# Gate rows as columns through DRAM, gate weights behind the filters, and inverse tables scaled on GpSimd, in a one-core AdaLN, spectral filter and SwiGLU block

## The chip, the cores and the metric

One core of a Trainium2 chip. The metric is the device time of one execution in microseconds (us). The kernel before takes 252.17 us (median of four runs, 251.6 to 252.89). An execution is called slow when it is over 1.5% above the fastest of the same kernel, otherwise fast. Each run also comes with the mean clock that the throttle granted TensorE.

## The reference, cut to what matters

```python
x = A_x                                                  # (1, 2048, 640), bf16
mod = (silu(c) @ w_mod).reshape(1, 6, 1, 640)            # w_mod (640, 3840)
sa, ca, ga, sb, cb, gb = mod[:, 0], ..., mod[:, 5]
h = layernorm(x) * (1 + ca) + sa
x = x + ga * irfft2(rfft2(h) * (w_r + 1j * w_i))         # the spectral half
h = layernorm(x) * (1 + cb) + sb
x = x + gb * ((silu(h @ w_gate) * (h @ w_up)) @ w_down)  # the gated half, FF = 1728
```

`ga` and `gb` are rows of 640 numbers. The kernel needs each on all 128 partitions: `ga` to scale the table `RI` of the inverse transform, `gb` to scale `w_down`. `sb` and `cb` are needed as columns (five groups of 128).

## The kernel before

Stages, with times of its profile: forward transform to 35.5 us; the spectral stretch, 21 groups of frequencies, each with products by the filters on VectorE, to 60.3 us; the change-over to 64.8 us; the inverse, 16 token tiles at a pitch of 1.1 us, to 82.3 us; then gate/up and down projections to 249.1 us. The first of five transposed tiles of the second layer norm (`h2T`) is made during the inverse: VectorE normalises two token tiles, the Sync queue issues a transpose by DMA, GpSimd and ScalarE multiply and add (`1+cb`, `sb`), and gate/up starts on it.

```python
# loads on the Sync queue, in order (cut)
#  ... wm_r[:, :, 0] (the ga weights, 800 KB), the filters Wv by way of DRAM, Ktab,
#  four DMA transposes of the spectral data, then:
nc.sync.dma_start(wm_r[:, :, 1:3, :], wm_m[:, :, 1:3, :])
nc.sync.dma_start(wm_r[:, :, 3, :], wm_m[:, :, 3, :])
nc.sync.dma_start(Htab[:], H_dram)
nc.sync.dma_start(RI[:], RI_dram)
#  ... w_down, the last columns of gate and up (Wp13), gate/up

def mod_bc(j, lo, bank, o=0, ks=range(NC5)):          # a gate row, on all partitions at once
    gps_ = psum[:, bank, o:o + 320]
    for k in ks:
        nc.tensor.matmul(gps_, lhsT=sc_rep[:, k, :], rhs=wm_r[:, k, j, lo:lo + 320], start=(k == 0), stop=(k == NC5 - 1))
    return gps_
# ga: two calls ahead of the first groups, copied by ScalarE to ga_bc [P, 4, 160]
# sb, cb: one-column products inside groups NG-4 .. NG-1, copied by VectorE

# the change-over
    if g == NG - 1:
        rot(40, 8, slice(0, 64), nc.vector, (1,))
        nc.vector.tensor_tensor(RI[:, 1], RI[:, 1], ga_bc[:], ALU.mult)      # fold 1
for l0, n, i in rots:
    rot(l0, n, slice(0, 64), nc.gpsimd, (i,))
nc.scalar.copy(gb_bc[:, 320:640], mod_bc(3, 320, 3, 128))
s1em(0); s1em(1)                                       # H-table products of tiles 0 and 1
for q0, q1 in ((0, 8), (8, 32), (32, 64)):
    rot(64, 16, slice(q0, q1), nc.vector)
nc.vector.tensor_tensor(RI[:, 0], RI[:, 0], ga_bc[:], ALU.mult)              # fold 0
```

`rot` multiplies by plus or minus one (a rotation by the imaginary unit). "Fold" below is the scaling of a half of `RI` by `ga`.

## Time and profile before

| kernel before, profiled run of 250.93 us, clock 1.0 | us |
|---|---|
| span | 249.12 |
| first filter product, last one ends | 37.81, 60.26 |
| first inverse matmul | 64.75 |
| first three gate/up loads issued | 63.0, 65.7, 67.7 |
| transpose of the first `h2T` tile issued, its first use | 71.83, 77.80 |
| first gate/up matmul, and from there to the end | 82.38, 166.74 |

This execution is 1.2 us faster than the median of the kernel before. The last row divides the kernel: what follows the first gate/up matmul is the same program before and after.

### The profile page before, as it was taken

The page shows a single profiled execution, that of the slowest core. Times are in us where ns is not written, and L with a number is a line of the kernel's source. Part 1 is how long each engine was busy: PE and PEld are TensorE (multiplying, and loading weights), DVE is VectorE, ACT ScalarE, POOL GpSimd, SP SyncE. Part 2 cuts the span into 40 slices and gives each one's busy share as a digit, 9 for nine tenths or more (in the row PEclk, how much of TensorE's full clock was granted, in tenths as well). Part 3 has the DMA queues.
Part 4 walks back from the last instruction along what each step waited for, and adds up shares of the span by engine and source line. Part 5 has one row for each costly group of instructions (what it writes and reads, how often), then busy time and mean ns, then how long its engine had stood idle before and what let it go on. Part 6 is the DMA issues. An engine that isn't in the chain of part 4 may idle for free.

```text
span 249.1 us, 6473 instructions
## 1 busy us (share of the span) xinstructions
PE 243.5 (98%) x2512; PEld 200.4 (80%) x2512; DVE 209.7 (84%) x524; ACT 162.7 (65%) x300; POOL 74.3 (30%) x122
## 2 busy tenths in 40 slices
PE   8999999999999999999999999999999999999994
PEld 3778877999889888688877778886768887779973
DVE  4798888998898997879997997879995888895895
ACT  3778666997788798488862487674356766235740
POOL 8487755894025422000003900001330000440000
PEclk9999999999999999999999999999999999999999
DMA  7999999999999999300005020003311000211001
GB/s 221 396 357 334 309 365 191 175 397 381 286 352 288 275 264 186 81 9 0 3 0 108 13 68 29 3 3 58 73 42 39 3 0 3 54 53 57 3 0 53
DMA packets 45760, 34.43 MB, mean 138 GB/s; under 512 B 21731, under 2 KB 42658, under 8 KB 45346
## 3 DMA queue, kind: packets, MB, share of 16 engines
q1 hardware_dynamic: 43936, 30.00, 42.8%
q0 software_dynamic: 1504, 3.95, 6.7%
q8 instruction: 19, 0.31, 0.5%
q10 hardware_dynamic: 290, 0.08, 0.1%
q14 instruction: 11, 0.09, 0.1%
HBM read 26.72 MB, written 4.72 MB: 126 GB/s over the span
## 4 chain that ended last, share of the span: by engine, by line
PE 80%; SPq 9%; DMA 6%; ACT 1%; DVE 1%; issue 1%; DVEq 0%; ACTq 0%
PE psum L1016 33%; PE psum L899 19%; PE psum L986 9%; DMA rW<-wflip_r 4%; PE psum L879 3%; PE psum L597 3%; PE psum L664 3%; PE psum L567 2%; SPq L273 2%; SPq L277 2%; PE psum L1149 2%; DMA rM<-in_w_mod_dram 2%; SPq L275 2%; PE psum L1152 2%; PE psum L974 2%; PE psum L618 2%
## 5 line engine op out<-in xcount | busy, mean ns | idle before, releaser
L1016 PEld LDWEIGHTS <-rW 128*128 128x128 bf16 (+1 forms) x528 | 46.9, 98 | 5.6 <-issue 0.2
L1016 PE MATMUL psum<-rW 128*128 128x256 bf16 (+1 forms) x240 | 27.1, 259 | 0.0
L913 POOL TENSOR_TENSOR rM<-rM,rL 128x320 f32<-128x320 f32 x6 | 5.9, 975 | 68.2 <-ACT rL L912 68.2
L899 PEld LDWEIGHTS <-rE 128*128 128x128 f16 (+1 forms) x196 | 19.1, 97 | 7.7
L1016 PE MATMUL psum<-rY,rW 128*128 128x256 bf16 (+1 forms) x96 | 24.0, 259 | 0.0
L986 PE MATMUL psum<-rW 128*128 128x256 bf16 (+1 forms) x170 | 23.1, 291 | 0.0
L899 PE MATMUL psum<-rE 128*128 128x320 f16 (+1 forms) x147 | 22.3, 299 | 0.0
L590 DVE TENSOR_TENSOR rM<-psum,rW 128x384 bf16<-128x384 f32 (+2 forms) x42 | 20.1, 541 | 2.0 <-PE psum L567 1.4
L986 PEld LDWEIGHTS <-rW 128*128 128x128 bf16 x170 | 16.6, 98 | 3.8
L1016 PEld LDWEIGHTS <-rE 128*128 128x128 f16 x192 | 17.4, 98 | 2.4
L899 PEld LDWEIGHTS <-rX 128*128 128x128 bf16 (+1 forms) x151 | 14.6, 97 | 5.4
L760 POOL TENSOR_TENSOR rstd<-rstd,mhalf 128x4 f32<-128x4 f32 (+2 forms) x4 | 4.5, 1120 | 48.2 <-DVE rstd L756 48.2
L1052 DVE TENSOR_TENSOR rH<-psum,rW 128x512 bf16<-128x512 f32 x21 | 14.5, 689 | 4.9 <-PE psum L1016 3.1
L1048 ACT COPY rH<-psum 128x512 f32<-128x512 f32 x21 | 12.3, 585 | 9.0 <-PE psum L1016 7.3
L1042 ACT COPY rW<-psum 128x512 f32<-128x512 f32 x21 | 12.3, 585 | 6.8 <-PE psum L1016 6.7
L1055 ACT COPY rX<-psum 128x512 f32<-128x512 f32 x21 | 12.3, 586 | 6.7 <-PE psum L1016 6.7
L1070 DVE TENSOR_TENSOR rX<-rH,rL 128x512 bf16<-128x512 bf16 x21 | 8.9, 423 | 9.1 <-ACT rL L1068 9.0
L382 DVE SCALAR_TENSOR_TENSOR rE<-rE,mv,psum 128x648 bf16<-128x648 f32 (+1 forms) x17 | 14.2, 844 | 2.1 <-PE psum L318 1.5
L1056 DVE TENSOR_TENSOR rX<-psum,rX 128x512 f32<-128x512 f32 x21 | 14.4, 685 | 1.7 <-ACT rX L1055 1.6
L899 PE MATMUL psum<-rA,rX 128*128 128x320 bf16 (+1 forms) x98 | 15.6, 299 | 0.0
L1016 PE MATMUL psum<-rH,rW 128*128 128x256 f16 (+1 forms) x96 | 15.1, 259 | 0.1
L1016 PE MATMUL psum<-rE,rY 128*128 128x256 f16 (+1 forms) x96 | 15.1, 259 | 0.0
(198 smaller groups left out, 674.3 us busy)
## 6 DMA issues: line engine op xcount, KB each, us to landing
out_dram<-rA SPq DMA_DIRECT2D x31, 80.0 KB, 1.6
rM<-in_w_mod_dram SPq DMA_DIRECT2D x3, 800.0 KB, 9.9
rX<-in_A_x_dram SPq DMA_DIRECT2D x3, 640.0 KB, 7.3
rA<-in_B_w_down_dram SPq DMA_DIRECT2D x2, 960.0 KB, 14.4
rM<-in_w_mod_dram SPq DMA_DIRECT2D x1, 1600.0 KB, 7.1
rY<-in_B_w_gate_dram POOLq DMA_DIRECT2D x2, 768.0 KB, 7.7
rW<-in_B_w_gate_dram SPq DMA_DIRECT2D x2, 640.0 KB, 7.2
rW<-in_B_w_up_dram SPq DMA_DIRECT2D x2, 640.0 KB, 6.5
```

The costliest lines, as they stand in the source:

```text
L382: nc.vector.scalar_tensor_tensor(Zv[:, h], Cv[:, h], mv[:, t, 0:1], zps[:, h], ALU.mult, ALU.subtract)
L590: nc.vector.tensor_tensor(PP[:, :, hl], xv[:, :, hl], in1, ALU.mult)
L597: nc.tensor.matmul(yps[:, i, :], lhsT=_rev(PP, 64 * n * ps + i, [[n, 128]]), rhs=identb[:], start=(ps == 1 and i == 0), stop=(ps == 0 and ...
L899: nc.tensor.matmul(o, lhsT=lhsT, rhs=rhs, start=start, stop=stop, skip_group_check=True)
L986: nc.tensor.matmul(gu[u], lhsT=Wgu[:, u, c5, ff * 128:(ff + 1) * 128], rhs=h2T[:, :, c5, :], start=(c5 == 0), stop=(c5 == NC5 - 1))
L1016: nc.tensor.matmul(o[:, f], lhsT=w, rhs=b, start=(start and f == 0 and i == 0), stop=(stop and f == F - 1 and i == len(ops) - 1), skip_gro ...
L1042: nc.scalar.copy(c0, X)
L1048: nc.scalar.copy(c2, X)
L1052: nc.vector.tensor_tensor(c11, Z, c0, ALU.add)
L1055: nc.scalar.copy(c3, X)
L1056: nc.vector.tensor_tensor(c22, Y, c3, ALU.add)
L1070: nc.vector.tensor_tensor(ato, v4(c11), v4(g21), ALU.mult)
```

## The change

The intent: less TensorE work for the gate rows, the filters earlier in the queue, and table scaling on an engine that had room. Each gate is made as a column with one-column products, transposed by TensorE to five rows of 128, written to DRAM, and read back to all partitions.

```diff
-    nc.sync.dma_start(wm_r[:, :, 0, :], wm_m[:, :, 0, :])      # ahead of the filters
 ...
     nc.sync.dma_start(Ktab[:, 0:384], K_dram[:, 0:384])
+    nc.sync.dma_start(wm_ga[:], wm_m[:, :, 0, :])              # behind the filters
+    nc.sync.dma_start(RI[:], RI_dram)
 ...  (behind the four transposes)
-        nc.sync.dma_start(wm_r[:, :, 1:3, :], ...); nc.sync.dma_start(wm_r[:, :, 3, :], ...)
-        nc.sync.dma_start(Htab[:], H_dram); nc.sync.dma_start(RI[:], RI_dram)
+        def g_write(i, eng):
+            eng.dma_start(g_dram[i][:], gT[:, i].rearrange("p a b -> p (a b)"))
+        def g_row(i, eng, row):
+            eng.dma_start(row[:], bass.AP(tensor=g_dram[i].tensor, offset=g_dram[i].offset, ap=[[0, P], [1, D]]))
 ...  (in stage_a)
+                    for c5 in {3: (0, 1), 7: (2, 3, 4), NG - 4: range(NC5)}.get(g, ()):
+                        mod_col(psum[:, b, 200 + c5:201 + c5], wm_ga if g < 8 else wm_r[:, :, 2], c5)
+                    if g in (9, NG - 2):
+                        nc.tensor.matmul(g_ps(b), lhsT=gcol[:, int(g > 9), :], rhs=identb[:], start=True, stop=True)
+            if g in (7, NG - 4):
+                nc.vector.tensor_copy(gcol[:, int(g > 9)], psum[:, b, 200:205])
+            if g in (9, NG - 2):
+                nc.vector.tensor_copy(gT[:, int(g > 9)], g_ps(b))
+                if g > 9:
+                    g_write(1, nc.gpsimd)
+            if g == 9:
+                nc.sync.dma_start(wm_r[:, :, 2, :], wm_m[:, :, 3, :])
+                nc.sync.dma_start(wm_r[:, :, 0, :], wm_m[:, :, 1, :])
+                g_write(0, nc.sync)
+                nc.sync.dma_start(wm_r[:, :, 1, :], wm_m[:, :, 2, :])
+                g_row(0, nc.sync, ga_bc)
+                nc.sync.dma_start(Htab[:], H_dram)
 ...  (change-over)
+            if g == NG - 3:
+                ri_fold(1)                                      # GpSimd, strided read of ga_bc
             if rots: rot(..., nc.gpsimd, ...)
+            if g == NG - 1:
+                rot(40, 8, slice(0, 64), nc.vector)
+                    if gs[0] >= NG - 2:                         # sb, cb behind the last third-stage pieces
+                        for c5 in range(NC5):
+                            mod_col(psum[:, 3, 192 + ...], wm_r[:, :, g - NG + 1], c5)
+        ri_fold(0)                                              # GpSimd
-        nc.scalar.copy(gb_bc[:, 320:640], mod_bc(3, 320, 3, 128))
-        s1em(0); s1em(1)
+        s1em(0); s1em(1); s1em(2)
+        g_row(1, nc.gpsimd, gb_bc)
         for q0, q1 in ((0, 8), (8, 32), (32, 64)):
             rot(64, 16, slice(q0, q1), nc.vector)
-        nc.vector.tensor_tensor(RI[:, 0], RI[:, 0], ga_bc[:], ALU.mult)
+        nc.vector.tensor_copy(modcols[:, 2:4, :], psum[:, 3, 192:202]...)
```

Some filter additions also move between VectorE and GpSimd; tile 0's inverse input is copied in two parts.

## The prediction

> **What bounds the kernel now.** I read the page first, then the chain of waits in order of time, then groups by shape, the instructions in order of time on each engine between 26 and 83 us, and the DMA packets per microsecond.
>
> ```profile
> PE 243.5 (98%) x2512; PEld 200.4 (80%) x2512; DVE 209.7 (84%) x524; ACT 162.7 (65%) x300; POOL 74.3 (30%) x122
> PE 80%; SPq 9%; DMA 6%; ACT 1%; DVE 1%; issue 1%; DVEq 0%; ACTq 0%
> ```
>
> TensorE holds 80% of the chain that ended last. Matmul ends are modelled, so I do not take the 98% as saturation; but the gaps that the waits show on PE are small, so outside the first 40 us the kernel is as long as PE's stream. Time comes from matmuls removed on the path, or from the few places where PE waits. The chain names both places that this change touches:
>
> ```profile
> 23.38 3.89 SPq L279
> 27.32 1.08 SPq L280
> ...
> 29.07 9.58 DMA rW<-wflip_r
> 38.74 0.44 DVE rW L407
> ...
> 60.63 0.41 ACT rY L600
> 61.12 0.59 ACT rY L600
> 61.76 0.40 PE psum L618 x4
> 62.16 0.68 PE psum L651 x5
> 62.84 0.97 PE psum L664 x16
> 63.81 0.22 PE psum L669 x4
> 64.04 0.68 PE psum L651 x5
> ```
>
> The columns are start and length in us. First place: the mirrored filters land at 38.65 us; a VectorE add and then the filter products wait for them, and from 39.2 to 44 us VectorE multiplies without a pause while PE waits for it twice (0.29 us each). The 800 KB of ga's weights (L279) stand in the queue just ahead of the filters. Second place: at 60.6 to 64.8 us, between the spectral stage and the inverse, the chain passes over two ScalarE copies, under which PE still has 12 small products to do and waits 0.26 us; then PE makes the gb row in two pieces of 0.68 us (L651), and waits 0.37 us for ScalarE before the first inverse matmul. From 65 to 82.5 us 17.5 us pass, with PE waits of some 0.1 to 0.2 us every third token tile. From 82.5 us on nothing changes.
>
> The shapes the change trades, from the groups by shape:
>
> ```profile
> L651 PE MATMUL psum<-rM,sc_rep 128*128 128x320 bf16 x20 | 3.5, 299 | 0.0
> L571 PE MATMUL psum<-sc_col,rM 128*128 128x1 bf16 x50 | 1.8, 163 | 0.0
> L407 POOL TENSOR_TENSOR rW<-rW 128x512 bf16<-128x512 bf16 x5 | 5.7, 1154 | 0.0
> L646 POOL TENSOR_SCALAR rE<-rE 128x512 bf16<-128x512 bf16 x13 | 7.8, 617 | 4.3 <-ACT rE L635 2.2 <-DVE rE L635 2.1
> L597 PE MATMUL psum<-identb,rM 128*128 128x128 bf16 x162 | 12.4, 219 | 0.0
> ```
>
> The 299 and 163 ns are latencies. The price is the spacing in the chain: five 320-column matmuls take 0.68 us, 137 ns each; ten one-column matmuls take 0.23 us and fifteen 0.35 us, 23 ns each; eight 128-column ones 0.45 us, 56 ns each.
>
> **What the Trainium skill says.** "TensorE: Matmul & The Clock Gate", section "Wait — 56ns, not 53.3ns?": spacing is N / 2.4 GHz plus about 2.5 ns, and start-to-start never drops below about 25 ns however small N is. The trace agrees: 137 ns for 320, 56 for 128, and 23 for one column, a little under that floor. So a gate row as 25 one-column products costs 0.58 us where the broadcast form costs ten times 137 = 1.37 us. "DMA: Bandwidth & Descriptors", section "Queues, rings and completion order": on each DMA engine, descriptors are consumed in ring order. The packets agree: the 640 packets of 1280 B of ga run from 28.3 to 32 us, and the 8 KB packets of the filters start only at 31.2 and thin out at 37.6. Same page, section "Two DMAs through the same engine are not ordered": a dependent DMA must wait for the first one's semaphore, so row to DRAM and back costs two latencies in series and blocks the issuing queue. "GPSIMD Engine Reference", section "3.1 Elementwise — side-by-side cycle accounting": about 2.6 cycles per element against VectorE's one. The trace: the same 128x512 add takes 1154 ns on GpSimd and 425 on VectorE.
>
> **The change part by part.**
>
> (a) PE work. Removed: 20 broadcast matmuls, 20 x 137 = 2.74 us. Added: 50 one-column products, 50 x 23 = 1.15 us, and two turns of a column block into five rows, 2 x 56 = 0.11 us. The 50 products for sb and cb only move, out of groups 17 to 20 to behind the last third-stage pieces. Net 1.48 us less PE work. But ga's half (1.37 us) ran at 35.9 to 39.5 us, while PE was waiting for the filters anyway, so only gb's 1.37 us lies on the path.
>
> (b) Filters earlier. Without ga's packets ahead (640 at about 285 per us, 2.2 us) the filters land near 38.65 - 2.2 = 36.4 us. What follows does not start 2.2 us earlier, because VectorE has its own queue: it ends the forward work at 35.5, then adds Wn 48:64 (0.42), waits to 36.4 for Wv 48:64 (0.43), adds Wn 0:16 (0.43), corrects two tile pairs (0.49) and adds Wn 16:32 (0.43), so products start near 38.1. Before, they ran gaplessly from 39.21 with one of 0.5 us already done, that is from 38.7. Gain 0.6 us. Group 5 is a second limit: its transpose by DMA landed about 41.2, and now ga's weights and the 320 KB inverse table are ahead of it, with the filters gone sooner: 0.9 us later by the packets. That allows group 5 near 42.4 instead of 42.6 to 43.1. I count 0.6 us.
>
> (c) Groups 5 to 20, 42.6 to 60.6 us, where PE and VectorE are nearly equal (17.9 and 16.4 us busy of 18). PE: -1.15 (sb, cb) + 1.15 (ga, gb) + 0.11. VectorE: four small copies of about 0.15 us. GpSimd: one more filter add (1.15 us). Loss about 0.15 us.
>
> (d) Change-over, 60.6 to 64.8 us. Both gb pieces go, -1.37. The 50 moved products are +1.15, of which some 0.25 us fits into the wait for ScalarE before the last group. VectorE loses two table scalings (2 x 0.48), two mod copies and the gb copy, and gains one rotation (0.28). Tile 0's VT copy is split, and the stages of three tiles instead of two are prepared before the first inverse, which hides the 0.37 us wait before the first inverse matmul. Sum: -1.37 + 1.15 - 0.25 - 0.37 = -0.84 us; I give back about 0.3 us for the GpSimd order under the rivals: -0.5.
>
> (e) Token tiles, 65 to 82.5 us: 16 x 1.105 = 17.7 us of work with inverse and column work together; VT ready two tiles ahead takes away perhaps 0.4 of the roughly 0.6 us of waits.
>
> Sum: -0.6 + 0.15 - 0.5 - 0.4 = -1.35 us. 252.14 - 1.35 = 250.8 us.
>
> **The rivals.**
>
> 1. GpSimd becomes the wait before the inverse. Its order near the end is: DMA of the gb row (0.5 to 0.8 us, as the small GpSimd DMAs took), a rotation (0.62), table fold 1 (estimate 640/512 x 1154 = 1.44 us), a rotation, fold 0 (1.44). The first cannot start until VectorE copies the gb row, near 58.7. That puts the last rotation near 62.1 us, just when PE would want it (62.2). If the gb copy or the folds are later or strided reads cost more, the inverse waits by 0.5 to 1.5 us and the total stays near 251.5 to 252. For: no slack. Against: GpSimd was idle 3.4 of the last 4.6 us before.
>
> 2. The row through DRAM blocks the Sync queue. The write of ga lies behind 1600 KB in the rings (4.1 us at about 400 KB per us), landing near 54.5; the read back waits for it, and the H table is issued behind that, at about 55, landing near 60.3, as before (60.4). It is wanted at 62.2. A miss would hold PE directly; another 2 us of latency would make 251.5 to 252.5. ga is back by 57, wanted by GpSimd at 59.
>
> 3. All of the filter gain arrives: if VectorE's adds overlap the landing and group 5's transpose is not late, (b) gives 1.2 to 1.5 us, and the total is near 250.
>
> 4. The filters were hidden anyway, and PE absorbs the head start in the balanced stretch (c): then only (d) and (e) remain, 251.4.
>
> **Range and chances.** The prediction is 250.8 us. The rivals span 250 to 252.5 us; the three runs before spread over 1.3 us by themselves. I take 249.6 to 251.9 as the range. A gain over 2% needs a time under 247.1, that is 5 us, more than all the PE waits and removed work between 36 and 82 us together (1.5 us of work net and 1.8 us of waits): 0.02. A loss over 2% needs over 257.2, which takes a Sync or GpSimd stall of 6 us: 0.02. Within 2%: 0.96.
>
> **What the changed profile would show.** (a) Twenty 320-column matmuls gone, 100 one-column ones at 23 ns. (b) The add that waits for the filters starts about 36.5 and products run from about 38.1; group 5 near 42.4. (d) Last spectral matmul near 60.1; first inverse matmul near 64.3 with three tiles prepared; no wait on GpSimd over 0.3 us before the first H-table matmul. (e) The first gate/up matmul of chunk 0 at 81.1 instead of 82.5; the rest, 166.6 us to the end, the same within 0.3 us. The prediction is wrong if PE waits for the H table, for the ga row or for GpSimd rotations by more than 0.7 us, or if the filters land early and group 5 then starts no sooner than before.

## More of the kernel before

The chain of waits (what released what, followed back from the end) of the kernel before passes from the inverse into gate/up on TensorE alone (start, length, what):

```profile
81.03 0.14 PE psum L1152 x2
81.44 0.55 PE psum L974 x5
82.54 1.53 PE psum L986 x14
```

L1152 is the inverse, L974 the small block that first uses the tile, L986 gate/up. There is no DMA in it: the tile is ready when TensorE comes to it.

## The result, and the profile after

255.55 us (median of four, 255.25 to 256.07) against 252.17: ratio 1.0135, 95% interval 1.0104 to 1.0166. Ratios here are the mean time of one kernel's fast runs over that of the other's of the same rounds, so not quite the ratio of the medians quoted. The class within 2% was right; the time lies 3.65 us above the upper end of the range, and its sign against before is wrong.

| | before | after |
|---|---|---|
| first product, last one ends | 37.81, 60.26 | 37.87, 60.51 |
| first inverse matmul | 64.75 | 67.38 |
| H table issued | 48.49 | 56.12 |
| first three gate/up loads issued | 63.0, 65.7, 67.7 | 65.8, 68.5, 70.9 |
| first tile: transpose issued, first use | 71.83, 77.80 | 74.49, 83.84 |
| first gate/up matmul | 82.38 | 86.82 |
| from there to the end | 166.74 | 166.66 |

The page of the kernel after, what the chain that ended last is made of:

```profile
PE 68%; DMA 8%; SPq 5%; ACT 1%; POOL 1%; issue 1%; DVE 0%; DVEq 0%; ACTq 0%; POOLq 0%
```

TensorE's share of the chain fell from 80 to 68%. The chain of waits, in order of time, shows where it left TensorE:

```profile
65.80 2.57 SPq L757
...
68.48 6.00 DMA rW<-in_B_w_up_dram
74.49 9.15 DMA rW<-rL
...
83.84 0.54 POOL rW L808
...
86.98 1.09 PE psum L1008 x10
```

SPq is the issuing Sync queue, DMA a transfer on its way, named by the memory regions of its target and source. From 57 to 84 us the chain passes over the Sync queue and its DMAs: the gate/up loads (L757), behind them the transpose of the tile (rW<-rL, 9.15 us), then the tile's scaling on GpSimd (L808), then gate/up (L1008). What had been ready in time became the last to arrive. When the transpose is issued is not set by the loads ahead of it: the queue has issued the last of them at 72.64, and the transpose goes out 0.02 to 0.03 us after VectorE has normalised the second token tile, before and then after (end at 71.81 and 74.46):

```profile
71.20 0.61 DVE L764 TENSOR_SCALAR rL<-rM,st,rstd 128x640 bf16<-128x640 f32 x1
```

```profile
73.85 0.61 DVE L786 TENSOR_SCALAR rL<-rM,st,rstd 128x640 bf16<-128x640 f32 x1
```

It is issued 7.1 us behind the first inverse matmul in both kernels. So the late issue (2.66 us) comes from the late inverse; what can come from the queue is that the tile then takes 9.35 us to its use instead of 5.97. TensorE's wait for the scaled tile (total, times, longest; before, TensorE has none here):

```profile
PE psum L996 <- POOL rW L808: 2.1, 4, 1.3
```

GpSimd's wait for the tile, in the waits, before and then after:

```profile
POOL rW L786 <- DMA rW<-rL: 7.1, 1, 7.1
```

```profile
POOL rW L808 <- DMA rW<-rL: 10.5, 1, 10.5
```

Why do the loads and the tile come late? The Sync queue in order of time (start, length, engine, line), before:

```profile
47.30 0.59 SPq L527 DMA_DIRECT2D rM<-in_w_mod_dram  x1
48.49 0.52 SPq L529 DMA_DIRECT2D rH<-tab_H  x1
...
62.98 2.57 SPq L735 DMA_DIRECT2D rW<-in_B_w_gate_dram  x1
...
71.83 1.79 SPq L778 DMA_TRANSPOSE rW<-rL  x1
```

and after:

```profile
48.22 0.58 SPq L597 DMA_DIRECT2D rM<-in_w_mod_dram  x1
...
49.93 0.40 SPq L600 DMA_DIRECT2D rM<-in_w_mod_dram  x1
55.73 0.34 SPq L534 DMA_DIRECT2D ga_bc<-ga_d  x1
56.12 0.43 SPq L602 DMA_DIRECT2D rH<-tab_H  x1
...
65.80 2.57 SPq L757 DMA_DIRECT2D rW<-in_B_w_gate_dram  x1
...
74.49 2.77 SPq L800 DMA_TRANSPOSE rW<-rL  x1
```

From 50.3 to 55.7 us the queue issues nothing: it waits for the gate row's write before it may read it back. The H table goes out 7.6 us later than before, and the gate/up loads behind it 2.8 us later or more. The packets of the trace say the same: without transposes, 17,843 KB had moved by 64 us before and 17,007 KB after; at some 360 KB per us that is 2.3 us. The DMA does not stand still while the queue is blocked, for it works off what was issued (352 to 389 KB in each microsecond from 51 to 55); the gap follows at 57, 58 and 59 us, with 142, 109 and 273 KB where the kernel before moved 432, 354 and 366. The row's own read falls into the same gap, and this profile does not separate the two.

A second new wait stands in the change-over. VectorE there, after (the number behind the comma is the length):

```profile
60.44 1.20 DVE L659 CAST rE<-psum 128x1024 bf16<-128x1024 f32 x1
61.67 3.21 DVE L670 TENSOR_SCALAR rE<-rE 128x512 bf16<-128x512 bf16 x2
```

and GpSimd in the same time:

```profile
61.15 1.42 POOL L694 TENSOR_TENSOR rH<-rH,ga_bc 128x640 bf16<-128x640 bf16 x1
62.53 0.61 POOL L670 TENSOR_SCALAR rE<-rE 128x512 bf16<-128x512 bf16 x1
63.12 1.40 POOL L694 TENSOR_TENSOR rH<-rH,ga_bc 128x640 bf16<-128x640 bf16 x1
```

Two rotations of 128x512 take 3.21 us, the first alone 3.01; before, one took 0.28 us:

```profile
62.39 0.28 DVE L646 TENSOR_SCALAR rE<-rE 128x512 bf16<-128x512 bf16 x1
```

The first ends at 64.68, just after GpSimd's second fold, at 64.52. TensorE waits 1.46 us for it:

```profile
PE psum L679 <- DVE rE L670: 1.5, 1, 1.5
```

The Trainium skill names a likely cause, and I had not drawn on it: "GPSIMD Engine Reference", section "1. Specifications", says that GpSimd's SBUF interfaces are shared with VectorE, with contention against VectorE instructions in a two-port mode or with two SBUF inputs. This trace agrees for the SBUF to SBUF rotation (0.28 us alone, 3.01 us under the folds); the neighbour that reads PSUM keeps its 1.20 us. That the rotation runs in a two-port mode no run here shows.

### The profile page after: what moved, and what is told of

Its sections match the earlier page's. It is cut to its first block, busy times and chain, and to the rows that moved or that the text cites. A ratio compares the mean times of both kernels' runs of the same rounds, so it can differ in the third digit from the quotient of the medians.

```text
span 253.5 us, 6555 instructions
## 1 busy us (share of the span) xinstructions
PE 243.2 (96%) x2544; PEld 200.1 (79%) x2544; DVE 213.2 (84%) x526; ACT 162.2 (64%) x298; POOL 77.5 (31%) x125
## 4 chain that ended last, share of the span: by engine, by line
PE 68%; DMA 8%; SPq 5%; ACT 1%; POOL 1%; issue 1%; DVE 0%; DVEq 0%; ACTq 0%; POOLq 0%
PE psum L1038 32%; PE psum L921 18%; PE psum L1008 9%; DMA rW<-rL 4%; PE psum L901 3%; DMA rL<-rA 2%; DMA rW<-in_B_w_up_dram 2%; PE psum L996 2%; SPq L747 2%; PE psum L581 2%; PE psum L621 1%; SPq L757 1%; POOL rW L808 1%; PE psum L642 1%; SPq L753 1%
## 5 line engine op out<-in xcount | busy, mean ns | idle before, releaser
L1008 PE MATMUL psum<-rW 128*128 128x256 bf16 (+1 forms) x170 | 23.1, 291 | 0.0
L1008 PEld LDWEIGHTS <-rW 128*128 128x128 bf16 x170 | 16.5, 98 | 3.8
L1175 DVE SCALAR_TENSOR_TENSOR rM<-psum,rX 128x640 f32<-128x640 f32 x16 | 13.1, 821 | 3.5 <-PE psum L1173 3.5
```

What stands on the lines that cost most here:

```text
L1008: nc.tensor.matmul(gu[u], lhsT=Wgu[:, u, c5, ff * 128:(ff + 1) * 128], rhs=h2T[:, :, c5, :], start=(c5 == 0), stop=(c5 == NC5 - 1))
L1175: nc.vector.scalar_tensor_tensor(x1[:, t, :].rearrange("p (m r) -> p m r", r=4), ops.rearrange("p r m -> p m r"), 1.0, x_sb[:, t, :].rearr ...
```

## The experiments

The expectations use letters. **L**: VectorE's rotation is held off by GpSimd's folds. **Q**: the Sync queue, blocked by the gate row, makes loads and tile late. "Narrow form" of L: only VectorE work whose source lies in SBUF is held off. **M**: the copy of the mod columns, last in VectorE's queue, holds back the inverse input because both lie in one PSUM bank. **T**: the `RI` load ahead of the transposes makes them late. **D** and **H**: the rows' way through DRAM costs DMA rate, H because 128 reads go to one DRAM row. **C**: the wait before gate/up halves the clock behind it. Milestones of all profiled runs are in one table; "gu" is gate/up, times in us.

| run | first inverse | first gu load | tile issued, used | first gu matmul | to the end | median | ratio to before, 95% |
|---|---|---|---|---|---|---|---|
| before | 64.75 | 63.0 | 71.83, 77.80 | 82.38 | 166.7 | 252.17 | |
| after | 67.38 | 65.8 | 74.49, 83.84 | 86.82 | 166.7 | 255.55 | 1.0135 [1.0104, 1.0166] |
| x1 | 66.80 | 65.8 | 73.91, 83.40 | 87.06 | 168.4 | 255.67 | 1.0136 [1.0068, 1.0203] |
| x2 | 66.98 | 64.1 | 74.65, 81.01 | 84.35 | 166.7 | 252.79 | 1.0052 [0.9984, 1.012] |
| x3 | 67.22 | 64.8 | 74.33, 82.49 | 85.70 | 166.6 | 253.82 | 1.0057 [1.0011, 1.0102] |
| x4 | 66.69 | 65.8 | 73.80, 81.59 | 84.90 | 166.7 | 253.89 | 1.0066 [1.0028, 1.0105] |
| x5 | 65.52 | 64.5 | 73.16, 81.54 | 84.84 | 167.4 | 254.14 | 1.0084 [1.0038, 1.013] |
| x6 | 66.15 | 65.7 | 73.26, 82.91 | 85.88 | 168.3 | 255.06 | 1.0102 [1.0027, 1.0178] |
| x7 | 69.31 | 67.6 | 76.41, 84.57 | 87.78 | 166.6 | 255.61 | 1.0145 [1.009, 1.02] |
| x8 | 66.56 | 65.5 | 73.67, 82.56 | 85.89 | 168.2 | 255.04 | 1.0101 [1.0047, 1.0156] |
| x9 | 66.27 | 63.9 | 75.47, 80.80 | 85.75 | 166.7 | 254.46 | 1.0114 [1.0084, 1.0144] |
| x10 (wrong result) | 65.33 | 64.2 | 72.44, 81.19 | 84.40 | 169.1 | 254.54 | 1.0106 [1.0034, 1.0179] |
| x12 | 66.59 | 65.6 | 73.69, 83.14 | 86.11 | 166.7 | 254.08 | 1.0080 [1.0055, 1.0105] |
| x14 | 67.87 | 65.7 | 75.25, 82.67 | 85.88 | 166.7 | 254.14 | 1.0075 [1.0054, 1.0097] |
| x15 | 65.96 | 64.6 | 73.05, 82.18 | 86.00 | 167.5 | 254.96 | 1.0095 [1.0037, 1.0152] |
| x17 | 67.11 | 65.1 | 75.13, 82.68 | 86.47 | 166.7 | 255.03 | 1.0138 [1.0096, 1.018] |
| x18 | 65.81 | 64.4 | 72.90, 82.24 | 85.43 | 167.5 | 254.31 | 1.0096 [1.0066, 1.0126] |
| x13 (before, plus reads) | 64.62 | 64.4 | 71.72, 79.32 | 82.64 | 167.5 | 251.97 | 1.0019 [0.998, 1.0059] |
| x16 (before, early `RI`) | 66.76 | 64.3 | 73.84, 78.97 | 84.39 | 166.8 | 252.62 | 1.0022 [0.9968, 1.0076] |

One profile is one execution, and the executions of one changed kernel spread by up to 4 us, so I lean on milestones for the mechanism and on ratios for the size. The intervals of x2 to x6 overlap, so the times alone do not rank these edits. One more thing moves milestones: in nine profiles of the table the trace holds stretches of 3.41 us at half the clock, starting at 64.77 in x2, 65.08 in x14, 65.63 in x17, 38.64 and 65.95 in x7, and between 83.97 and 86.00 in x1, x6, x8, x10 and x15. The 167.4 to 167.5 us to the end of x5, x13 and x18 are not explained by it. All runs gave the right result except x10.

### x1: folds on VectorE

```diff
-            nc.gpsimd.tensor_tensor(RI[:, i], RI[:, i], ga_bc..., ALU.mult)
+            nc.vector.tensor_tensor(RI[:, i], RI[:, i], ga_bc..., ALU.mult)   # behind the rotations, not among them
```

> The changed kernel with the two inverse-table folds put back on VectorE (0.48 us each), all else kept. Theory L (a VectorE rotation of 128x512 cannot run while GpSimd works through its folds): the rotation pair takes about 0.5 us instead of 3.2, the first inverse matmul comes near 64.9 us instead of 67.4. If L alone is the loss, the first gate/up matmul of chunk 0 comes near 82.3 and the kernel takes 251.5 to 252. Theory Q (the Sync queue, blocked 5.4 us by ga's way through DRAM, issues all later loads some 3 us late, so that the normalised tiles' transpose lands late): L's wait goes but a wait of 2 to 3 us for the transposed tiles stays before the gate/up stage, first gate/up matmul near 84.5, 253 to 253.8.

The rotations are back at 0.30 and 0.29 us, and the second H-table matmul moves from 65.03 to 63.89: the lock is gone. The total is not better (255.67). The gain ends at the mod columns' copy, which the two folds (now 0.82 us each, because `ga_bc` is read with a stride; 0.48 before) push to 65.95, and the late tile sets the end anyway. The inverse and the tile's issue both come 0.58 us earlier, yet the tile still takes 9.5 us from issue to use: an inverse earlier by this little does not cure the slow tile.

### x2: the H table issued ahead of the read-back

```diff
                 nc.sync.dma_start(wm_r[:, :, 1, :], wm_m[:, :, 2, :])
-                g_row(0, nc.sync, ga_bc)
                 nc.sync.dma_start(Htab[:], H_dram)
+                g_row(0, nc.sync, ga_bc)
```

> The changed kernel with the H table issued on the Sync queue before ga's read-back instead of after it; the folds stay on GpSimd. Theory Q: the loads after it are issued sooner, the wait for the transposed tiles before gate/up shrinks from 3.6 us in all to under 1; the rotation still takes 3.2 us and the first inverse matmul stays near 67.4; 253 to 254. If L is all and the late transpose only follows from the late inverse stage: no change, 255.3 to 255.7.

One line moved, and the ratio falls from 1.0135 to 1.0052, some 2.1 us (2.8 in the medians, 255.55 to 252.79). The queue still waits for the row, to 55.6 us, but 1 MB of H table is now in the queue ahead of the wait: 17,566 KB by 64 us instead of 17,007. Loads come 1.7 us earlier, the tile is used 6.36 us after its issue instead of 9.35, although it is issued no earlier, and gate/up starts 2.5 us earlier. TensorE no longer waits for the tile at all, so in this profile the edit takes that wait away, as Q says. The rest of the delay stays: the lock was still there, with the late fold now on the six small rotations (2.69 us in place of 1.04), and this profile also has its stretch of half clock in the change-over. That Q is the larger part of the time is not shown: x4, which leaves the queue as it is, has 1.0066, and the intervals overlap.

### x3: both

```diff
 both edits above, x1 and x2
```

> Both edits. L and Q together: first inverse matmul near 64.9, first gate/up matmul near 82.2, 251.3 to 252.2, the kernel before within half a per cent. If a third cause is at work it stays over 252.8.

Not the sum: 253.82. Both cures are seen (rotations 0.30 and 0.29, H table at 50.8) and yet the inverse starts at 67.22. VectorE's order shows why; the mod columns' copy stands behind everything:

```profile
64.69 1.04 DVE L670 TENSOR_SCALAR rE<-rE 128x128 bf16<-128x128 bf16 x6
65.65 0.82 DVE L694 TENSOR_TENSOR rH<-rH,ga_bc 128x640 bf16<-128x640 bf16 x1
66.38 0.16 DVE L739 COPY modcols<-psum 128x10 f32<-128x10 f32 x1
```

### x4: the rotation reads PSUM

```diff
-                rot(40, 8, slice(0, 64), nc.vector)
+                src = banks(6, 2, [8, 128]).rearrange("p i (q c) -> p q c i", c=2)   # the same data, before the copy
+                for i in range(2):
+                    nc.vector.tensor_scalar(E1[:, :, 1 - i, :], src[:, :, i, :], 1.0 - 2.0 * i, 1.0, ALU.mult, ALU.mult)
```

> The changed kernel with the rotation of columns 40 to 47 reading the PSUM banks that the copy before it read, instead of the SBUF result of that copy; the folds stay on GpSimd at the same place. Theory L in its narrow form[...]: from PSUM the pair takes about 1.3 us although GpSimd is folding; the first inverse matmul near 65.5, total as x1 or 0.3 us more (253.2 to 254). Rival: VectorE is slowed by any GpSimd work, or it waits for something else at that point: the pair still ends near 64.8 us and nothing changes (255.5).

This takes the SBUF source away and leaves the folds where they are. VectorE in the change-over of x4:

```profile
61.77 1.27 DVE L726 TENSOR_SCALAR rE<-psum 128x512 bf16<-128x512 f32 x2
62.97 0.67 DVE L654 CAST rE<-psum 128x512 bf16<-128x512 f32 x1
63.74 2.19 DVE L670 TENSOR_SCALAR rE<-rE 128x128 bf16<-128x128 bf16 x6
```

Under a fold that runs from 61.66 to 63.08 the two rotations from PSUM take 0.67 us each, not 3.01. The six small ones that still go from SBUF to SBUF, under the fold from 63.63 to 65.03, take 2.19 us where they take 1.04 alone. So the lock holds for the source in SBUF and not for PSUM: L is shown, in the narrow form. TensorE now waits 0.59 us for something else, the H table, which lands at 64.08; the first inverse matmul gains 0.69 us.

### x5: x3 with the mod columns' copy ahead of the last rotations

```diff
+        nc.vector.tensor_copy(modcols[:, 2:4, :], psum[:, 3, 192:202]...)      # before the rotations of 64..79
         for q0, q1 in ((0, 8), (8, 32), (32, 64)): rot(64, 16, ...)
-        nc.vector.tensor_copy(modcols[:, 2:4, :], psum[:, 3, 192:202]...)      # after them
```

> Third theory M: in x3 (folds on VectorE, H table first) the first inverse matmul still came at 67.2 us, because the matmuls of the fifth filter row write the PSUM bank from which VectorE copies the mod columns, and that copy now stands last in VectorE's queue, behind the rotations and both folds. This is x3 with the mod-column copy moved ahead of the last rotations. M: the first inverse matmul comes near 65.7 us, total 0.5 to 1.2 us below x3. Rival: the folds on VectorE (0.82 us each here, not 0.48) are the chain by themselves, then the first inverse matmul stays above 66.8 and the total equals x3.

The first inverse matmul comes 1.70 us earlier than in x3 (65.52): M is shown for the order of the copy; that the shared bank is the reason is what the wait of the inverse input for the mod columns suggests (0.3 us in the changed kernel, 1.5 in x3); no run isolates it. The total does not follow (254.14); the tile is used only at 81.54, and it is the tile that gate/up waits for.

### x6: the row goes first

```diff
             if g == 9:
+                g_write(0, nc.sync)
                 nc.sync.dma_start(wm_r[:, :, 2, :], ...)
+                g_row(0, nc.sync, ga_bc)
                 nc.sync.dma_start(wm_r[:, :, 0, :], ...); nc.sync.dma_start(wm_r[:, :, 1, :], ...)
                 nc.sync.dma_start(Htab[:], H_dram)
# folds on GpSimd while VectorE still multiplies out of PSUM (57.66 and 60.29 us); mod columns as in x5; write of gb later
```

> All three causes mended with the folds still on GpSimd: ga's row goes to DRAM ahead of the three big weight loads and comes back behind the first of them; fold 1 and fold 0 then run while VectorE multiplies from PSUM (57.6 to 61.6 us), the gb row goes to DRAM after the rotations, and the mod-column copy stands ahead of the last rotations. L, Q and M together: ga back before 55 us, rotation pair 0.5 us, first inverse matmul near 65.2 with three tiles ready, no wait over 0.5 us for the transposed tiles, first gate/up matmul near 82.0, 251 to 251.8 (before 251.9). If folding on GpSimd costs VectorE time wherever it stands, products end later than 60.8 and the total is 252.5 or more.

The read-back is issued at 49.81 without a block, and L and M are mended (rotation pair 0.56 us). The gate/up loads are as late as in the changed kernel all the same (65.7). So a blocked queue is not all of it. The packets show a slump: 162 and 192 KB in the microseconds from 53 and 54, where the row is read back as 128 pieces of 1280 B, against 366 to 376 around it; and again from 69 to 71 us, where gb comes back (32 packets of 5120 B, median 0.89 us). The H table needs 12.9 us to land, and TensorE waits 0.67 us for it.

### x7: x6 with `RI` loaded behind the transposes

```diff
-        nc.sync.dma_start(RI[:], RI_dram)          # ahead of the transposes
+                nc.sync.dma_start(RI[:], RI_dram)  # behind the first gate load of x6
```

> x6 with the inverse table (320 KB) loaded behind the first transposes instead of ahead of them. Theory T (the head start of the filters is lost because the DMA transposes queue behind the moved loads): the corrections of groups 5 and 9 on GpSimd come 0.5 to 0.9 us earlier than in x6 and the products end 0.3 to 0.5 us earlier. Rival: the transposes are limited by themselves; nothing moves.

Everything came later (products end at 62.09, clock 0.985 in the profiled run, with a stretch of half clock from 38.64 on, among the products). It gave T no support and, at that clock, does not refute it.

### x8: x6 with the small gate copies on ScalarE

```diff
-                nc.vector.tensor_copy(gcol[...], psum[:, b, 200:205]);  nc.vector.tensor_copy(gT[...], g_ps(b))
+                nc.scalar.copy(gcol[...], psum[:, b, 200:205]);         nc.scalar.copy(gT[...], g_ps(b))
```

> x6 with the four small copies of the gate columns and rows (0.16 and 0.27 us each on VectorE) on ScalarE. If VectorE sets the pace of the spectral groups, the products end 0.4 to 0.7 us earlier than in x6 and the total falls by as much; if PE does, or if ScalarE's copies become the wait, nothing or the opposite.

The products end at 61.58 instead of 60.65, 0.93 us later: ScalarE has no room either. The four copies are not a cause that moving them cures. One of its four runs, 258.35 us, was slow; the median of the three fast ones is 254.14.

### x9: no DRAM at all

```diff
+        def diag(i):      # gate column times identity, on GpSimd
+            nc.gpsimd.tensor_tensor(dg[i], identb broadcast to [P, 5, 128], gcol broadcast to [P, 5, 128], ALU.mult)
+        # ones (128x128) times dg: the row on all partitions, in PSUM; three pieces at groups 18 to 20 for ga,
+        # two in inverse tiles 3 and 4 for gb; ScalarE copies; ga_bc in [4, 160] order again
-        g_write, g_row
```

> Edit: the changed kernel with the gate rows made without DRAM: the gate column times the identity on GpSimd gives a diagonal table, and ones times that table on the tensor engine gives the row in PSUM (three pieces behind the last product stages for the first gate, two pieces in the inverse for the second); folds contiguous again (one on GpSimd under VectorE's PSUM copies, one on VectorE); mod columns copied before the last rotations. The filters stay in front of the gate weights. Theory D (the trip of the gate rows through DRAM costs DMA rate and lands the gate/up loads and the transpose late): first gate/up loads issued 63.0 to 64.0 us (changed 65.8), transposed tile 6.0 to 6.8 us after its issue (changed 9.35), first gate/up matmul 82.0 to 83.5 us, time 250.5 to 252.5, ratio to before 0.995 to 1.003. Rival E (the loads are late because the order of the queue changed, gate weights and inverse tables in other places, not because of the rows): loads still at 65 or later and the transpose 8 us or more, first gate/up matmul 85 to 86.5, ratio 1.008 to 1.014.

The DMA side is as D expects: loads at 63.9, no slump, and the tile's packets done at 78.58, 3.1 us after the issue. The rest failed: ScalarE's copies delay the last groups, and the gb pieces cost two waits of 1.25 and 0.78 us in the inverse, so the tile is issued at 75.47 and gate/up starts at 85.75. The milestone for the loads was met, the times for gate/up and for the total were missed; the cure cost what it saved.

### x10: x6 with the rows read from 128 different DRAM rows (wrong result)

```diff
-            eng.dma_start(row[:], bass.AP(tensor=g_dram[i].tensor, offset=g_dram[i].offset, ap=[[0, P], [1, D]]))
+            eng.dma_start(row[:], bass.AP(tensor=w_mod.tensor, offset=w_mod.offset, ap=[[6 * D, P], [1, D]]))
```

> Edit: the row-first kernel (x6) with both gate rows read from 128 different DRAM rows of the weight table instead of one row 128 times; wrong result on purpose, the writes stay. Theory H (128 descriptors on one DRAM address are what is slow): packets of these 1280-byte reads take about as long as other loads (under 300 ns, against up to 1159 ns), no dip of the rate at the read-back, H lands under 9 us after its issue (12.87 in x6), first gate/up loads before 64.3 us, transpose under 7.5 us, time 252 to 253.5. Rival I (the address doesn't matter, the small descriptors and their place in the queue do): loads at 65 to 66, transpose about 9 us, time 254.5 to 255.5 as x6.

The slump at the read-back is gone (391 and 371 KB in the microseconds from 53), gb's packets take 0.36 us instead of 0.89, loads start at 64.2 instead of 65.7. The tile still takes 8.75 us and the median is no better than x6's within its spread. The address matters for the rate; its price in time is not shown by this run.

### x11 and x13: idle one-row reads in the kernel before

```diff
+        def hot_row(i, eng):
+            eng.dma_start(hot, bass.AP(tensor=w_mod.tensor, offset=w_mod.offset, ap=[[0, P], [1, D]]))
+        hot_row(0, nc.sync)                       # ahead of the H table
         nc.sync.dma_start(Htab[:], H_dram)
 ...
         s1em(0); s1em(1)
+        hot_row(1, nc.gpsimd)
```

> Edit: the kernel before with two idle reads added that nothing uses: one DRAM row of 1280 bytes read to all partitions on the Sync queue ahead of the H table, and the same on the GpSimd queue where the changed kernel reads the second gate row. No write and no wait goes with them. Theory H: the first gate/up loads move from 63.0 to 64.5 or later, the transpose lands 7.5 us or more after issue, first gate/up matmul 83.5 to 85.5 against 82.4, ratio to before 1.005 to 1.012. Rival I and rival W (only the write and its wait hurt): loads within 0.5 us of before, first gate/up matmul under 83, ratio 0.998 to 1.003.

x11 took 273.0 us and tells nothing of this: I had put its target into space where TensorE's first spectral table is written, and that write waited 21 us for the read. x13 is the same with a free target.

> Edit: the kernel before with two idle one-row reads, as in x11 but into space that no table of the products uses (in x11 the target was the space of the first table, which had to wait for the read). H: rate under 250 KB per us for a microsecond or two behind the H issue, first gate/up loads 64.0 to 65.5 against 63.0, transposed tile 7 us or more after issue, first gate/up matmul 83.2 to 85.0, ratio 1.003 to 1.011. Rival I: loads at 63.0 to 63.7, first gate/up matmul under 82.9, ratio 0.998 to 1.003.

The rate drops to 95 KB in the microsecond from 56, the loads come at 64.4 instead of 63.0 and the tile takes 7.6 us instead of 5.97: H is right about the mechanism, the loads inside its range. The time is 1.0019 [0.998, 1.0059], first gate/up 82.64: in the kernel before there is slack for it, and H's ranges for that matmul (83.2 to 85) and for the ratio (1.003 to 1.011) were missed. So one-row reads cost DMA time by themselves, but not the 1.35%.

### x12 and x14: a mended kernel, with 16 copies of the row and with one

```diff
 x6, with: RI loaded behind the transposes; read-back behind the second gate load; H table ahead of the last gate load;
           both folds behind the last GpSimd rotation; mod columns' copy behind the first two rotations
-    g_dram = [dram.tile([NC5, 128], ...)]
+    g_dram = [dram.tile([16, D], ...)]            # x12 only: written 16 times, each read by 8 partitions
```

> Edit: the changed kernel mended in every place named so far: each gate row written to DRAM in 16 copies and read back 8 partitions to a copy, the inverse tables loaded behind the transposes again, the write first and the read-back behind the second gate load, the H table before the last gate load, both folds on GpSimd ahead of VectorE's SBUF rotations, mod columns copied after the first two rotations. If H (one DRAM row read 128 times is slow) and the named waits are the whole cause: transposes of the spectral stretch issued out by 47.5 us, no microsecond under 300 KB between 51 and 64, first gate/up loads 63.2 to 64.2 us, first inverse matmul 64.6 to 65.6, transposed tile under 6.8 us after issue, first gate/up matmul 82.3 to 83.6, time 251 to 252.7, ratio 0.997 to 1.004. If something else delays it: first gate/up matmul over 84.2, ratio over 1.006.

> Edit: x12 with one row in DRAM, read 128 times, as in the changed kernel; nothing else differs. H: a dip to under 250 KB per us at the read-back and again where the second gate row comes back, gate/up loads 0.8 to 1.6 us later than in x12, first gate/up matmul 0.8 to 2.5 us later, ratio 0.004 to 0.01 above that of x12. Rival I: loads and ratio within 0.3 us and 0.003 of x12.

x12 has no slump (no packet of the read-back over 0.16 us; 351 KB in its slowest microsecond from 53 to 58), x14 has one (89 KB from 56), and their times are 254.08 and 254.14: H's price in this kernel is below what can be seen, and its ranges for the loads and the ratio were missed. x12 missed its time (251 to 252.7) for reasons of my own making: the last gate load landed after TensorE wanted it (a wait of 1.21 us), the folds stood under the rotation again (1.41 us for one), and loading `RI` later left the DMA 753 KB behind the kernel before at 64 us.

### x15: the corrected sum

```diff
 x12, with: RI ahead of the transposes; one load for the two mod gates, ahead of the H table; folds as in x6;
+        VTs = {0: s1er(0)}
+        for i in range(10):
+            mod_col(psum[:, 7, 192 + i:193 + i], wm_r[:, :, i // 5], i % 5)    # behind the first inverse input, other bank
```

> Edit: x12 with what its run showed wrong put right: inverse tables loaded ahead of the transposes as in the changed kernel, the two mod gate columns' weights in one load ahead of the H table (2560-byte pieces), folds on GpSimd where x6 had them (in VectorE's PSUM stretch), mod columns computed behind the first inverse input instead of in front of it and in another bank. Rows in 16 copies. If the causes named (late loads, lock, mod columns, row) are the whole loss: gate/up loads 63.2 to 64.3 us, rotation pair under 0.7 us, first inverse matmul 64.3 to 65.6, transposed tile under 7 us after its issue, first gate/up matmul 82.0 to 83.8, time 250.8 to 252.8, ratio 0.996 to 1.004. If not: first gate/up matmul over 84.2 and ratio over 1.006.

The rotation pair is mended (0.68 us), loads come at 64.6 (a miss by 0.3), the first inverse matmul at 65.96 (a miss by 0.4) and the tile takes 9.13 us: gate/up at 86.00, median 254.96. Mending the named causes together does not bring the kernel back. Its six runs differ oddly, though: 252.08 and 254.15 us at clock 1.0 and 0.998, 254.75 to 255.62 at 0.993.

### x16: the kernel before with `RI` ahead of the transposes

```diff
         nc.sync.dma_start(Ktab[:, 0:384], K_dram[:, 0:384])
+        nc.sync.dma_start(RI[:], RI_dram)
 ...
-        nc.sync.dma_start(RI[:], RI_dram)          # behind the H table
```

> Edit: the kernel before with the inverse tables loaded ahead of the transposes of the spectral stretch, and nothing else. Theory T (this load is what makes the transposes and all behind them late in the changed kernel): last of the four transposes issued out by 48.1 us or later against 47.25, gate/up loads 0.3 us or more later, time up 0.3 to 1 us. Rival (it only fills an idle stretch, x12 points that way): transposes within 0.4 us of before, gate/up loads 0.3 to 0.9 us earlier (62.1 to 62.7), time within 0.5 us of before or below it.

The last of the four transposes, in the Sync queue of x16:

```profile
44.99 4.42 SPq L520 DMA_TRANSPOSE rM<-rA  x1
```

It is out at 49.41, where the kernel before is through with it at 47.25 and the changed kernel at 48.17. In this profile the load alone makes transposes, products (they end at 62.27) and loads 1.3 to 2.2 us late, as T expects; the time says 1.0022 with an interval that includes no change, so T is neither shown nor refuted in the time, and small. It also contradicts x12 in part, where the load stood behind the transposes and they were out at 48.38 all the same.

### x17 and x18: idle matmuls in the wait before gate/up

```diff
             if t == NT - 1:
+                idle_pe(4)                        # four 512-column matmuls that nothing reads
                 fin13 = gu13(0, at_of(0))
 ...  in gu13, first tile only:
+            if ci == 0 and c5 < 4:
+                idle_pe(1)
```

x17 is the changed kernel with this, x18 is x15 with it.

> Edit: the changed kernel with idle matmuls (ones times ones, nothing reads them) put on the tensor engine where it waits for the transposed tile: four of 512 columns ahead of the first piece of the 64-row gate/up block, one after each of its first four pieces. Theory C (in most runs of the changed kernels the wait ahead of gate/up halves the granted clock for some 3.4 us behind it, which costs about 1.7 us and shows as a mean clock of 0.993 and a stretch from the first gate/up matmul to the end of 168.3 in place of 166.7 us): clock 0.997 or more in at least five of six runs, the stretch to the end 166.6 to 167.0, median 254.0 to 255.0. Rival (the clock doesn't depend on that wait, or the fill only adds work): clock 0.993 in half the runs or more and median 255.3 to 256.5.

> Edit: x15 with the same idle matmuls. x15 took 252.08 and 254.15 us in its two runs at clock 0.998 or more, and 254.75 to 255.62 in its four at 0.993. Theory C: clock 0.997 or more in at least five of six runs, median 252.2 to 253.8, ratio 1.001 to 1.007. Rival: clock 0.993 in half the runs, median 254.5 to 256.0, ratio over 1.009.

The reason for them lies in x15's windows (stretch, busy time of TensorE, its weight loads, VectorE, ScalarE and GpSimd with counts, granted clock, DMA share, GB per s):

```profile
82.00:86.00 4.00, 2.35 (x11) 1.48 (x12) 2.38 (x8) 0.98 (x2) 3.81 (x6) 0.75 1.08 358
86.00:90.00 4.00, 4.00 (x33) 3.36 (x32) 3.15 (x9) 2.47 (x6) 2.01 (x3) 0.83 1.09 276
```

TensorE is busy for 2.35 of 4 us while it waits for the tile, and the clock falls to 0.75 and 0.83 of full on average over the two stretches; the trace holds it as one stretch of 3.41 us at 0.5 from 83.97 on. With the fill, in x18:

```profile
82.00:86.00 4.00, 3.45 (x24) 1.94 (x22) 2.64 (x7) 0.98 (x2) 3.76 (x6) 1.00 1.08 358
```

The Trainium skill has the mechanism in "TensorE: Matmul & The Clock Gate", section "Part 1: The HAM clock gate (the "warmup" mystery)": the clock is halved after a free-running window of about 3.4 us that was idle, and comes back after a busy one. The traces agree in the length: every stretch of half clock in these profiles is 3.41 us long. Half of that is lost, 1.7 us, or 0.7% of the span, which is a mean clock of 0.993. The runs agree in the size: 0.993 is what many runs of the changed kernels show, and of the stretches to the end in the table those with the dip behind the tile (x1, x6) are 168.3 and 168.4 us against 166.7. They differ in the threshold: in the 3.41 us before these stretches TensorE was busy for 1.2 to 2.7 us, so no fully idle window was needed, and x12 and the changed kernel waited as long (2.1 to 2.2 us in all) at full clock.

C's prediction for the clock came true in x18: 0.998 or more in six of six runs, against two of six in x15. In x17 it held in three of six only; its profile has the dip from 65.6 to 69.0 us, behind the wait in the change-over, which was not filled. The times did not follow: the medians fell by 0.65 us in x18 (254.31; I had said 252.2 to 253.8) and by 0.5 in x17 (255.03), but the kernel before was faster in these rounds too, and the ratios to it are unchanged (1.0096 against 1.0095 for x15, 1.0138 against 1.0135). That the clock costs time is not shown by the fill, which also adds work to the wait. A kernel at full clock is not yet back at the time before.

## Why the prediction was wrong, point by point

The terms of the prediction's sum against the milestones of the two profiles, in us (before to after; these milestones differ by 4.36 in all and the medians by 3.38, so some 1 us is scatter of the profiled runs):

| term | predicted | measured |
|---|---|---|
| (b) and (c), to the end of the products | -0.45 | +0.25 |
| (d) change-over, to the first inverse matmul | -0.5 | +2.38 |
| (e) token tiles, to the first gate/up matmul | -0.4 | +1.81 |
| from there to the end | 0 | -0.08 |

Two steps failed: (d), where VectorE became the wait, and (e), where gate/up came to wait for the first transposed tile, which no step of the prediction looked at.

**(a) TensorE work.** The counts are as worked out, and TensorE is 0.3 us less busy in the page. It bought nothing, because neither half of it lay where TensorE sets the end after the change.

**(b) Filters earlier.** The landing was right: the addition that waits for the filters starts at 36.10 (said 36.5; before 38.74), and products run from 37.87 (said 38.1). The gain of 0.6 us was not: the end of the products is 60.51 against 60.26. Group 5 and group 9 take their input from the transposes by DMA, which begin no earlier (36.81 against 36.76): both times the first goes out 0.03 us after one of ScalarE's last copies into its source region. The first three then take 8.16 us to issue instead of 6.94, and the gate weights and `RI` still move where the DMA had run nearly dry before (82 KB in the microsecond from 37); that this is the reason was not shown (x7, x16). The second transpose is used at 46.04, 45.76 before. The prediction named this limit for group 5 and did not follow it to group 9.

**(c) The spectral stretch.** 0.15 us was allowed; the head start of this stretch is lost in it and 0.25 us more. ScalarE has no slack to take the copies either (x8).

**(d) The change-over.** This step failed, with the largest error of the sum: -0.5 predicted, +2.38 measured, which puts the first inverse matmul 2.63 us late. Rival 1 looked at the right place and put 0.5 to 1.5 us on GpSimd being late; GpSimd was not late, it held VectorE off: 1.46 us of TensorE's wait is the rotation under the folds, shown by x1 and x4. Taking the lock away alone moves the first inverse matmul by only 0.6 to 0.7 us, because the copy of the mod columns, last in VectorE's queue, then sets it; moving that copy is worth another 1.7 us (x3 against x5). The late inverse delays the tile's issue by the same amount. A smaller error: the 0.37 us before the first inverse matmul that this step hoped to hide was idle time of the weight loads; between the matmuls themselves the pause was 0.20 us.

**Rival 2, the Sync queue.** Issue times were near what it said (read-back at 55.73, H table at 56.12), but the H table landed at 63.31, not near 60.3. That is 0.04 us before TensorE's first use of it, so in the changed kernel it was only just early enough; x4, where the lock is gone, waits 0.59 us for it. What the rival did not ask is what stands behind the H table in the same queue: the gate/up loads, 2.8 us later, which are still on their way when the transpose of the first tile is issued. x2 moves one line, and gate/up starts 2.5 us earlier in its profile; by the ratios it is 0.8% faster, with intervals that overlap a little (from 1.0104 to 1.012).

**(e) Token tiles.** The pitch of 1.1 us was right, and no waits are left between the tiles: the inverse up to its last tile took 0.91 us less than before, more than the 0.4 predicted. But this step failed in what follows: it let gate/up follow from the inverse, and it followed from the tile, which costs 2.72 us there. Predicted first gate/up matmul 81.1, measured 86.82. With the tile as quick as before, a sum from these traces (74.49 + 5.97 us, and 2.2 us of scaling) has it ready at 82.7, before the inverse is through (83.16): an estimate that needs the slow tile for the wait, and not only its late issue. The 9.35 us from issue to use is partly the transpose itself: its 1280 packets take 2.97 us from first to last before, 4.98 after, 1.92 in x9; the first of them starts 2.27, 3.49 and 1.19 us after the issue. In the changed kernel 43 packets take over 0.2 us, and they end in two groups: 20 begun from 78.46 to 79.66 end within 0.02 us of 80.73, and 22 begun from 81.31 on end near 82.85; before, 24 packets end together near 76.30; in x9 none does this. So they wait for something common, and no run shows what.

**Beyond 86.82: the clock.** Three of the four runs of the changed kernel have a clock of 0.992 or 0.993; of 50 runs of the kernel before one has. No step of the prediction had a clock in it. The profiled run of the changed kernel was its one run at 1.0, and at 255.25 us it is only 0.2 to 0.8 us faster than the other three, so the clock is a small part of the 3.4 us.

**What stays open.** No changed kernel came back to 252 us in the median; the best is x2, whose interval includes equality. x15 removes the block, the lock and the copy, and its tile still needs 9.13 us. So the slow tile has a cause that stays open: x1 and x4 have the same times for the loads (65.8) and the issue (73.9 and 73.8), and use the tile 9.49 and 7.79 us later. Why a tile's transpose takes 5 us in one kernel and 2 in another I can't say. H is shown as a mechanism of the rate (x6 against x10, x12 against x14, x13) and no effect of it on the time could be seen (x12 against x14).

## What to carry to other kernels

A wait on an issuing queue is paid by everything behind it: when a DMA has to wait for another, ask for the whole list of later transfers which of them has the least slack, and put independent loads in front of the waiting one. An elementwise job moved to GpSimd did not slow VectorE here while VectorE read PSUM (0.67 us a rotation in x4); against VectorE's work between SBUF and SBUF it made three microseconds of a 0.3 us instruction. And when a wait of the chain looks like one queue's doing, check what released the last instruction of the queue: here the transpose's issue followed VectorE, not the loads ahead of it. A wait of TensorE that is new can be followed by a slower clock, in some executions only (168.3 us to the end instead of 166.7), so look at the granted clock of every run and not of the profiled one alone.

## What the Trainium skill lacked or had wrong

- "GPSIMD Engine Reference", section "1. Specifications", names the contention with VectorE, and no page that I found says how long VectorE is held when GpSimd instructions follow one another without a pause. Here a 128x512 bf16 rotation from SBUF to SBUF went from 0.28 to 3.01 us under three GpSimd instructions in a row (61.15 to 64.52 us), ending 0.16 us after the last; the same rotation from PSUM took 0.67 under a fold.
- "TensorE: Matmul & The Clock Gate" gives an idle window as the condition for the halved clock. Here nine profiles have such stretches behind 3.41 us in which TensorE was busy for 1.2 (x1) to 2.7 us (x2), and the changed kernel's profile, with a window of 1.3 us, has none.
- "DMA: Bandwidth & Descriptors" says nothing that I found on many reads of one DRAM row: 128 descriptors of 1280 B from one row took the rate from about 370 to 89 to 192 KB per us for a microsecond or two; from 16 copies the read-back took no packet over 0.16 us and never fell below 351.
- The same page has no figure for a transpose by DMA next to other loads: 1280 packets took 1.92 us in x9, 2.97 in the kernel before and 4.98 in the changed one.
